# A third split product in two of eight steps, high parts at the ends of cycles, early transforms one product later, two last sends on GpSimd's queue

## The chip, the cores and the metric

One core of one Trainium2 chip runs the whole program. The time is the device time of one execution in microseconds; three executions of the kernel before took 1777.51, 1778.03 and 1778.36 us, so its median is 1778.03 us.

## The reference

```python
X = np.fft.fft(x, axis=1)          # x: (8, 3008, 256) float32
X = np.fft.fft(X, axis=2)
x = X.real.reshape(24064, 256)
h = x @ w_in                       # w_in: (256, 2048)
g = h * np.clip(h + 3.0, 0.0, 6.0) / 6.0
out = g @ w_out                    # w_out: (2048, 256)
```

A two-dimensional Fourier transform over positions and channels is followed, on its real part, by a two-layer network with a hard swish between the layers. All data are float32.

## The kernel before, in words

**The pieces.** The 3008 positions are 47 times 64. `stage1` (L327) transforms over the 47, `stage2` (L563) over the 64, and the transform over the channels is folded into `w_in`. Images go in four pairs, and each pair has 12 chunks of at most 256 columns, so there are 48 chunks. The last chunk of each pair (`ch.last`) has 192 columns in the second layer. A chunk has 8 steps, one for each 256 columns of the hidden layer; `fc` counts them from 0 to 7. Step number s is 8 times the chunk plus `fc`.

**First layer.** From step 22 on, a `Unit` computes 512 columns of the first layer: `passes` (L717) multiplies split parts of the transform (tile KQ) with split parts of the weights (KW) into a bank `u`, first the even half (128 rows, `blk` 0), later the odd half (127 rows, `blk` 1). Between them ScalarE keeps the even sums (`s<-u`, L741) because the odd half goes on adding into the same bank. VectorE then makes the other sign (`v<-s,u`, L751), ScalarE two Relu (`t`, L791), VectorE two gates (`A<-t`, L794).

**Second layer.** It is a Strassen-like scheme: GpSimd combines the four gated blocks of a step (`c`, L809), and `mlp2` (L865) makes seven products i = 0 to 6 into four `acc` banks, 256 columns each. A product in float32 is written in the trace as two matmul records. From chunk 8 on (`CHUNK2`), products 0 and 1 are made of three fp32r matmuls instead: high part, low part and rest of the moving data (tile J, written by `split_gates`, L882 to L893) times high parts of the weights (GH) or their low parts and rests (GK). `THIRD = (4,)` adds product 2 of step 4 of every chunk: `split_third` (L895 to L905) writes tile J3 with two operations on ScalarE (`J<-A` 256 at L900, `high<-J` 256 at L903) and two on VectorE (L904, L905), and the product becomes three fp32r matmuls from J.

**Order.** Nothing is scheduled by a tool; the program is written in cycles by the loop at the end of the kernel. From chunk 8 on one cycle is one step and one unit: odd half of a unit, product 0, product 1, even half of the next unit, any `stage2`, then the other products. Work on the other engines is put between. In a cycle with a `stage1`, its matmuls stand `behind_it` products before the cycle's end: 1 where the step before held a `stage2`, else 2. `third_high()` issues the first operation of a third in the cycle before the step, `third_others()` the other three at the end of that cycle. `split_weights` (L908) makes GK; `keep_high` (L922 to L927) turns the weights GH from float32 to their high parts by two operations on ScalarE through a bank, once per step of chunk 7 that is done, in the middle of a cycle. While one of the two is under way `lent` is set, and `split_gates` then takes bank y0 (shared with `v` and with `split_third`) instead of y1.

**The end.** The last chunk's results go out in `send` (L1026): two tiles of eight DMAs each, alternately issued from SyncE and ScalarE.

**The start.** FI (row indices, a column of signs, and 16-bit tables E) is loaded once, on ScalarE's queue, into a tile that lives through the program.

Of the kernel before, what the change touches and what calls it, by code (L numbers as in the profile page):

```python
# [60 lines left out]
def kernel(  # L61
# [67 lines left out]
    CHUNK2, NFR = 8, 2  # L129
    THIRD = (4,)  # L130
    SPLIT = CHUNK1 * NF - 2
# [5 lines left out]
    F1 = consts.tile([P, 5 * PB], F32, name="F1")  # L137
    FI = consts.tile([P, NIX + 1 + P], F32, name="FI")
    IX = FI[:, 0:NIX].bitcast(I32)
# [4 lines left out]
    G = consts.tile([P, 6 - NFR, NF, P], F32, name="G")  # L144

    def split_products(fc):
        return NFR + (fc in THIRD)

    GH = [consts.tile([P, split_products(fc), P], F32, tag=f"GH{fc}", name="GH") for fc in range(NF)]
    G2 = {fc: consts.tile([P, P], F32, tag=f"G2{fc}", name="G2") for fc in range(NF) if fc not in THIRD}  # L150

    def weight(i, fc):
        if i == NFR and fc in G2:
            return G2[fc][:]
        return GH[fc][:, i] if i <= NFR else G[:, i - NFR - 1, fc]
    half = consts.tile([P, 1], F32, name="half")
# [486 lines left out]
    def split_q(ch, ps):  # L643

        x = ps[:, :, 0:ch.nq]
        high, low, rest = (KQ[:, j, :, ch.n_all % 3, 0:ch.nq] for j in range(3))
        ch.row = qpool.tile([P, TB], F32, tag="row", name="row")
        nc.scalar.mul(high, x, 1.0 - EPS / 2.0)
        nc.scalar.copy(ch.row[P - DH:P, 0:ch.nq], ps[P - DH:P, 1, 0:ch.nq])

        def low_part():
            nc.vector.scalar_tensor_tensor(low, x, 1.0, high.bitcast(F32), op0=AL.mult, op1=AL.subtract)
# [177 lines left out]
    def split_of(ch, fc):  # L830
        return ch.n_all >= CHUNK2

    def order_of(ch, fc):

        if not split_of(ch, fc):
            return [[(i, None)] for i in range(7)]
        high, others = ([(i, j) for i in range(NFR)] for j in (HIGH, OTHERS))
        rest = [[(i, ALL if i < split_products(fc) else None)] for i in range(NFR, 7)]
        if ch.final and fc >= NF - LAST:
            return [high, others] + [rest[i - NFR] for i in (3, 5, 6, 4, 2)]  # L840
        if fc in THIRD:
            rest = rest[1:3] + rest[0:1] + rest[3:]
        order = [high] + rest[:2] + [others] + rest[2:]
        while len(order) > 7:
            order[0:2] = [order[0] + order[1]]
        return order

    def mlp2(ch, fc, lo, hi):
        a = ch.a[fc].rearrange("p m f n -> p (m f) n")[:, :, 0:ch.n]
        c = ch.c[fc]  # L850
        moving = [a[:, 0], a[:, 1], a[:, 3], c[:, 0], c[:, 1], c[:, 2], c[:, 3]]
        order = order_of(ch, fc)
        if fc == NF - 1 and lo == 0:
            ch.e = epool.tile([P, 5, TB], F32, tag="e", bufs=1, name="e")
            if ch.final:
                ch.e2 = epool.tile([P, 2, TB], F32, tag="s", bufs=1, name="e")
        for i, parts in (x for part in order[lo:hi] for x in part):
            if fc == 0 and i % 2 == 0 and parts != OTHERS:
                ch.acc[i // 2] = ps_a.tile([P, 2, TB], F32, tag="acc", name="acc")
            o = ch.acc[i // 2][:, i % 2, 0:ch.n]  # L860
            for j in parts or (None,):
                assert (j is None) != (weight(i, fc).dtype == F32R)
                w = weight(i, fc) if not j else GK[fc][:, j - 1, i]
                x = moving[i] if j is None else J3[:, j, 0:ch.n] if i == NFR else parts_tile(ch, fc)[:, j, i, 0:ch.n]
                nc.tensor.matmul(o, w, x,  # L865
                                 start=(fc == 0 and i % 2 == 0 and j in (None, 0)), stop=(fc == NF - 1),
                                 skip_group_check=True)
# [42 lines left out]
    def split_weights(fc):  # L910

        low, rest = (GK[fc][:, k] for k in range(2))
        ps = bank([P, split_products(fc), P], "high")
        nc.scalar.mul(low, GH[fc][:], HIGH_PART)
        nc.vector.tensor_scalar(ps[:], low.bitcast(F32), 1.0 / EPS, None, op0=AL.mult)
        nc.vector.scalar_tensor_tensor(low, GH[fc][:], (1.0 + EPS) / EPS, ps[:], op0=AL.mult, op1=AL.subtract)
        nc.vector.scalar_tensor_tensor(ps[:], ps[:], -EPS, low.bitcast(F32), op0=AL.mult, op1=AL.add)
        yield
        nc.vector.tensor_scalar(rest, ps[:], 1.0 / (1.0 + EPS), None, op0=AL.mult)

    def keep_high(fc):

        ps = bank([P, split_products(fc), P], "high")
        nc.scalar.copy(ps[:], GH[fc][:])
# [92 lines left out]
    def send(ch, o, m):  # L1017
        if not ch.final:
            for j, (bj, k1) in enumerate(ch.blocks[m]):
                nc.sync.dma_start(out=out_k[ch.pr.p, k1, bj], in_=o[:, j].rearrange("p h e -> p (h e)"))  # L1020
            return
        for j in (slice(0, 4), slice(4, 6)):
            (b0, k1), (b1, _) = ch.blocks[m][j][:2]
            rows = out_k[ch.pr.p, k1, b0::b1 - b0]
            for q in range(P // DH):
                (nc.sync, nc.scalar)[q % 2].dma_start(  # L1026
                    out=rows[:, q].rearrange("b i e -> i b e"),
# [74 lines left out]
    def join(j):  # L1102
# [7 lines left out]

        outs = GH[2 * n + i][:, 0:NFR], G[:, B12 - NFR - 1:B22 - NFR:B22 - B12, 2 * n + i]
        for h, o in enumerate(outs):
# [3 lines left out]
    def mix_w_out(j):  # L1116

        g = {i: G[:, i - NFR - 1, 2 * j:2 * j + 2, :] for i in range(NFR + 1, 7)}
        tt = nc.gpsimd.tensor_tensor
# [4 lines left out]
        for k in range(2):  # L1124
            tt(weight(2, 2 * j + k), g[5][:, k], GH[2 * j + k][:, B21], op=AL.subtract)

# [30 lines left out]


    def load_table():
        nc.sync.dma_start(out=F1[:], in_=c_stage1[:, 8 * PB:13 * PB])  # L1160
# [14 lines left out]
    load_w(0, nc.sync)  # L1175
    nc.scalar.dma_start(out=F[:], in_=c_stage1[:, 0:8 * PB])
    nc.scalar.dma_start(out=FI[:], in_=c_stage1[:, 13 * PB:])
    zero = QN[PB:PX, 2]
# [125 lines left out]
    def beside():  # L1304
# [50 lines left out]
    def open_slots():  # L1355
        nonlocal A, GK
# [3 lines left out]
        GK = [slots.tile([P, 2, split_products(fc), P], F32R, tag=f"GK{fc}", name="GK") for fc in range(NF)]  # L1360

# [4 lines left out]

    epool = jpool = KW = A = GK = J = J3 = None
    steps = [(p, ck, fc) for p in range(NP) for ck in range(NCK) for fc in range(NF)]
# [256 lines left out]
    seed(units[1])  # L1625
    weights_of, rested, kept = list(range(NF)), 0, 0

# [3 lines left out]

    thirds = [s for s in gates_of if steps[s][2] in THIRD]
    third = []

    def third_high():

        if thirds and not third and thirds[0] <= now[0] + 1:
            ch, fc = chunk(thirds.pop(0))
# [50 lines left out]
    while done < len(stream):  # L1689
# [18 lines left out]
        third_high()  # L1708
        if not un:
            third_others()  # L1710

# [56 lines left out]
        flush(high_of)  # L1768
        third_others()
        for gen in parts:  # L1770
            next(gen, None)
# [112 lines left out]
```

## Time and profile before

| what | value |
|---|---|
| median of three executions | 1778.03 us (1777.51 to 1778.36) |
| the profiled execution's own time | 1779.34 us |
| its span, first to last instruction | 1777.5 us |
| granted TensorE clock | 0.999 |
| idle of TensorE ahead of a matmul, named waits, whole program | 2.2, 1.6, 0.9, 0.8, 0.6, 0.5, 0.5, 0.3 us |
| GpSimd's `c` waiting for `acc` products | 330.5 us in 247 waits |

The profiled execution took 1.3 us more than the median, so a sum of pieces of it is a difference to be taken from either. Matmuls are pipelined and their ends are modelled, so the table of busy time says little here: a matmul that starts late because of a wait inside the row is still drawn as busy. What a step costs is read from the starts of equal rows in consecutive cycles.

### The profile page before, as it was taken

The numbers are of one execution on the slowest core, as the hardware profiler recorded it, in microseconds if no ns is written. First come the engines' busy times: TensorE is split into PE (matmuls) and PEld (weight loads), VectorE is DVE, ScalarE is ACT, GpSimd is POOL, SyncE is SP. The second block draws the span as 40 slices with busy tenths as digits, with TensorE's granted clock in tenths as the row PEclk, the third lists the DMA queues.
The fourth block names the chain that finished last, engine by engine and source line by source line (L and its number), as shares of the span: only waits on it lengthen the run. The fifth ranks groups of instructions, "written<-read, shape, count | busy, mean of one in ns | idle before, by whom it ended". The sixth has DMA issues, their size and how long they took to land.

```text
span 1777.5 us, 30218 instructions
## 1 busy us (share of the span) xinstructions
PE 1764.3 (99%) x9632; PEld 1518.3 (85%) x9632; DVE 1494.5 (84%) x2868; ACT 1411.4 (79%) x2573; POOL 1312.7 (74%) x1474
## 2 busy tenths in 40 slices
PE   8999999999999999999999999999999999999998
PEld 6688888888988888888998888888899888888897
DVE  8988676668988888888898888888899888888887
ACT  6556666678888888888888888888888888888885
POOL 5687777776678787886768878887766766776675
PEclk9999999999999999999999999999999999999999
DMA  8433332312113222121112222321111111101101
GB/s 281 121 93 99 103 78 70 85 37 51 37 48 81 71 64 78 47 73 43 30 44 64 70 78 57 86 64 37 48 36 34 37 21 48 41 19 45 21 13 34
DMA packets 160811, 110.39 MB, mean 62 GB/s; under 512 B 122562, under 2 KB 141344, under 8 KB 160652
## 3 DMA queue, kind: packets, MB, share of 16 engines
q1 hardware_dynamic: 151900, 82.22, 18.5%
q0 software_dynamic: 7504, 25.65, 4.7%
q8 instruction: 76, 1.25, 0.3%
q14 instruction: 83, 0.68, 0.1%
q10 hardware_dynamic: 1248, 0.59, 0.1%
HBM read 71.93 MB, written 36.79 MB: 61 GB/s over the span
## 4 chain that ended last, share of the span: by engine, by line
PE 95%; DVE 2%; ACT 2%; issue 0%; DMA 0%; another core or an unknown queue 0%; DVEq 0%; ACTq 0%
PE acc L865 58%; PE u L717 27%; PE ps L563 2%; PE ps L327 2%; PE acc L819 1%; PE v L613 1%; PE u L613 1%; ACT t L791 1%; PE spare L1138 0%; DVE v L751 0%; PE ps L526 0%; PE ps L395 0%; PE awake L1165 0%; DVE J L892 0%; ACT PM L1069 0%
## 5 line engine op out<-in xcount | busy, mean ns | idle before, releaser
L865 PE MATMUL acc<-c,G 128*128 128x256 f32 (+1 forms) x3008 | 766.7, 376 | 0.0
L717 PE MATMUL u<-KQ,KW 128*128 128x512 f32 (+7 forms) x2376 | 743.8, 426 | 1.0 <-ACT s L741 0.6
L809 POOL TENSOR_TENSOR c<-A 128x512 f32<-128x512 f32 (+1 forms) x359 | 453.9, 1264 | 337.3 <-PE acc L865 328.5
L865 PEld LDWEIGHTS acc<-c,G 128*128 128x128 f32 x3008 | 533.1, 189 | 80.3 <-issue 12.8
L717 PEld LDWEIGHTS u<-KQ,KW 128*128 128x128 f32 (+1 forms) x2376 | 426.1, 189 | 67.0 <-ACT s L741 3.0
L791 ACT ACTIVATE t<-u,half 128x512 f32<-128x512 f32 (+1 forms) x384 | 261.9, 682 | 169.9 <-PE u L717 111.7
L791 ACT ACTIVATE t<-v,half 128x512 f32<-128x512 f32 (+1 forms) x384 | 262.3, 683 | 106.1 <-DVE v L751 104.5
L751 DVE SCALAR_TENSOR_TENSOR v<-s,u 128x512 f32<-128x512 f32 (+1 forms) x360 | 247.0, 686 | 117.5 <-ACT t L791 111.6
L809 POOL TENSOR_TENSOR c<-c,A 128x256 f32<-128x256 f32 (+1 forms) x359 | 260.4, 725 | 28.2
L809 POOL TENSOR_TENSOR c<-A,c 128x256 f32<-128x256 f32 (+1 forms) x359 | 260.2, 725 | 28.2
L794 DVE SCALAR_TENSOR_TENSOR A<-t,v 128x512 f32<-128x512 f32 (+3 forms) x481 | 250.2, 541 | 36.7 <-ACT t L791 34.1
L865 PE MATMUL acc<-J,GK 128*128 128x256 f32 (+1 forms) x1340 | 270.7, 322 | 1.4 <-DVE J L905 0.8
L892 DVE SCALAR_TENSOR_TENSOR J<-high,A 128x512 fp32r<-128x512 f32 (+1 forms) x315 | 211.2, 670 | 55.8 <-ACT high L891 45.4
L794 DVE SCALAR_TENSOR_TENSOR A<-t,u 128x512 f32<-128x512 f32 (+3 forms) x481 | 248.4, 537 | 0.0
L732 ACT ACTIVATE u<-QN,WN 128x512 f32<-128x512 f32 (+1 forms) x324 | 224.8, 694 | 0.0
L865 PEld LDWEIGHTS acc<-J,GK 128*128 128x128 f32 x1340 | 204.7, 189 | 17.5 <-DVE J L893 1.6
L893 DVE SCALAR_TENSOR_TENSOR J<-high,A 128x512 fp32r<-128x512 f32 (+1 forms) x315 | 210.5, 668 | 0.0
L886 ACT ACTIVATE J<-A 128x512 fp32r<-128x512 f32 (+1 forms) x315 | 193.4, 614 | 0.0
L891 ACT COPY high<-J 128x512 f32<-128x512 f32 (+1 forms) x315 | 185.2, 588 | 4.9 <-DVE KQ L893 2.4
L741 ACT COPY s<-u 128x512 f32<-128x512 f32 (+2 forms) x315 | 180.3, 572 | 9.5 <-PE u L717 8.3
L865 PE MATMUL acc<-A,G 128*128 128x256 f32 (+1 forms) x630 | 184.6, 375 | 0.0
L865 PEld LDWEIGHTS acc<-J,GH 128*128 128x128 f32 x670 | 125.8, 189 | 24.1
(184 smaller groups left out, 1808.5 us busy)
## 6 DMA issues: line engine op xcount, KB each, us to landing
out_dram<-o SPq DMA_DIRECT2D x744, 32.0 KB
T<-in_c_stage_dram SPq DMA_DIRECT2D x26, 512.0 KB
g<-zd SPq DMA_DIRECT2D x42, 256.0 KB
zd<-z SPq DMA_DIRECT2D x48, 192.0 KB
QN<-qd SPq DMA_DIRECT2D x43, 128.0 KB
xt<-in_x_dram SPq DMA_DIRECT2D x21, 256.0 KB
st<-in_moe_w_out_dram POOLq DMA_DIRECT2D x7, 512.0 KB
xt<-in_x_dram SPq DMA_DIRECT2D x17, 192.0 KB
```

The costliest lines, as they stand in the source:

```text
L717: nc.tensor.matmul(un.wide(un.u[:]) if un.joint else un.u[:, i, 0:un.nq], un.weights(j, blk, i, rows), un.moving(j, blk, rows), start=Fals ...
L732: nc.scalar.activation(un.wide(un.u[:]), un.wide(row), AF.Identity, scale=WN[:, f:f + 1])
L741: copy(un.wide(un.s[:]), un.wide(un.u[:]))
L751: nc.vector.scalar_tensor_tensor(v, s, -2.0, u, op0=AL.mult, op1=AL.add)
L791: nc.scalar.activation(t, h, AF.Relu, bias=half[:], scale=scale)
L794: nc.vector.scalar_tensor_tensor(dst, t, 1.0, h, op0=AL.min, op1=AL.mult)
L809: (eng or nc.gpsimd).tensor_tensor(out, in0, in1, op=AL.add)
L865: nc.tensor.matmul(o, w, x, start=(fc == 0 and i % 2 == 0 and j in (None, 0)), stop=(fc == NF - 1), skip_group_check=True)
L886: nc.scalar.mul(high, a, 1.0 - EPS / 2.0)
L891: nc.scalar.copy(ps, high.bitcast(F32))
L892: nc.vector.scalar_tensor_tensor(low, ps, -1.0, a, op0=AL.mult, op1=AL.add)
L893: nc.vector.scalar_tensor_tensor(rest, ps, 1.0 + EPS, a, op0=AL.mult, op1=AL.subtract)
```

## The change

It has six parts.

1. `THIRD` becomes (3, 5), and the new `third_of` leaves out the last chunks. Product 2 is split in two steps of 36 chunks instead of one step of 40. The order within such a step is as it was for step 4. Weights for it are made by `split_third_weights` into three tiles GK3 of their own, after the eight `split_weights`.
2. `keep_high` is called at the end of a cycle, at most twice, after product 1 of the step concerned has been issued, and uses bank y0; it no longer sets `lent`.
3. `behind_it` is 1 in all steps below 62.
4. The last two of the eight last sends are issued from GpSimd.
5. FI is put in a tile that is freed after step 7, and `load_index` loads its indices and signs again, on SyncE's queue in step 2, into a small tile `signs`.
6. The one-row copy that is spread over the partitions is written straight into QN, and the layout of the weight tiles changes (G2 goes into G, GK is one tile). `third_high()` is also called from `third_others()`, and the early call of `third_others()` in cycles without a unit goes.

```diff
-    THIRD = (4,)
+    THIRD = (3,5)
...
-        ch.row = qpool.tile([P, TB], F32, tag="row", name="row")
+        ch.row = QN[:, ch.n_all % 4]
...
+    def third_of(ch, fc):
+        return split_of(ch, fc) and fc in THIRD and not ch.last
...
-        if fc in THIRD:
-            rest = rest[1:3] + rest[0:1] + rest[3:]
+        rest = [[(i, None)] for i in range(NFR, 7)]
+        if third_of(ch, fc):
+            rest = rest[1:3] + [[(NFR, ALL)]] + rest[3:]
...
+    def split_third_weights(fc):
+        yield from split_parts(weight(NFR, fc), bank([P, P], "high")[:], *(GK3[fc][:, j] for j in range(3)))
...
     def keep_high(fc):
 
-        ps = bank([P, split_products(fc), P], "high")
+        ps = ps_u.tile([P, NFR, P], F32, tag="y0", name="high")
         nc.scalar.copy(ps[:], GH[fc][:])
-        GH[fc] = consts.tile([P, split_products(fc), P], F32R, tag=f"GH{fc}", name="GH")
+        GH[fc] = consts.tile([P, NFR, P], F32R, tag=f"GH{fc}", name="GH")
         nc.scalar.mul(GH[fc][:], ps[:], HIGH_PART)
-        yield
...
-        for j in (slice(0, 4), slice(4, 6)):
+        for i, j in enumerate((slice(0, 4), slice(4, 6))):
...
-                (nc.sync, nc.scalar)[q % 2].dma_start(
+                (nc.sync, nc.scalar, nc.gpsimd)[2 if m == i == 1 and q > 1 else q % 2].dma_start(
...
+    def load_index():
+        nonlocal FI, IX
+        FI, IX = signs, signs[:, 0:NIX].bitcast(I32)
+        nc.sync.dma_start(out=FI[:], in_=c_stage1[:, 13 * PB:13 * PB + NIX + 1])
...
+        put(2, load_index)
...
     def third_others():
+        third_high()
         for gen in third:
             next(gen, None)
...
-        if not un:
-            third_others()
...
-        if kept < NF and not stages and not ends and done >= 7 * ((CHUNK2 - 1) * NF + kept - SPLIT) + 7:
-            splitting, kept = keep_high(kept), kept + 1
-            next(splitting)
-        elif weights_of and not stages and not ends and not closing and rested >= 3:
-            splitting, rested = split_weights(weights_of.pop(0)), 0
+        if weights_of and not stages and not ends and not closing and rested >= 3:
+            (f, fc), rested = weights_of.pop(0), 0
+            splitting = f(fc)
             next(splitting)
...
-        behind_it = 1 if any(s - 1 in middle_fns for s in begun) else 2
+        behind_it = 1 if any(s - 1 in middle_fns or s < CHUNK2 * NF - 2 for s in begun) else 2
...
         third_others()
+        for _ in range(2):
+            if kept < NF and not stages and not ends and done >= 7 * ((CHUNK2 - 1) * NF + kept - SPLIT) + NFR:
+                keep_high(kept)
+                kept += 1
```

What this does to the order of instructions shows in three places.

TensorE, two neighbouring steps of a usual chunk (here chunk 17), from the step's even half of the first layer (the L717 row) on. Before, steps 3 and 4; the products of `c` are those with GpSimd's combinations, J those with split data:

```order
L717 MATMUL u<-KQ,KW 128x512 x3
L865 MATMUL acc<-c,G 128x256
L865 MATMUL acc<-J,GK 128x256 x4
L865 MATMUL acc<-c,G 128x256 x3
L717 MATMUL u<-KQ,KW 128x512 x3
L865 MATMUL acc<-J,GH 128x256 x2
L865 MATMUL acc<-c,G 128x256
L717 MATMUL u<-KQ,KW 128x512 x3
L865 MATMUL acc<-c,G 128x256
L865 MATMUL acc<-J,GK 128x256 x4
L865 MATMUL acc<-J,GH 128x256
L865 MATMUL acc<-J,GK 128x256 x2
```

Now step 3 and the start of step 4:

```order
L709 MATMUL u<-KQ,KW 128x512 x3
L863 MATMUL acc<-c,G 128x256
L863 MATMUL acc<-J,GK 128x256 x4
L863 MATMUL acc<-J,GK_1680 128x256 x3
L863 MATMUL acc<-c,G 128x256 x2
L709 MATMUL u<-KQ,KW 128x512 x3
L863 MATMUL acc<-J,GH 128x256 x2
L863 MATMUL acc<-A,G 128x256
```

The three extra fp32r matmuls now follow the four of products 0 and 1 in step 3 (and again in step 5), and step 4 has its product 2 in float32 once more (the row `A,G`).

ScalarE, from the end of chunk 8's step 2 to the end of its step 3. `high<-GH` and `GH<-high` are `keep_high`, `J<-A` 256 and `high<-J` 256 the third. Before:

```order
L924 COPY high<-GH 128x256
L926 ACTIVATE GH<-high 128x256
L891 COPY high<-J 128x512
L732 ACTIVATE u<-QN,WN 128x512
L791 ACTIVATE t<-u,half 128x512
L886 ACTIVATE J<-A 128x512
L900 ACTIVATE J<-A 128x256
L791 ACTIVATE t<-v,half 128x512
L741 COPY s<-u 128x512
L924 COPY high<-GH 128x256
L926 ACTIVATE GH<-high 128x256
L891 COPY high<-J 128x512
```

Now, from the last two `keep_high`, at the end of step 0 of that chunk, to the end of step 1:

```order
L724 ACTIVATE u<-QN,WN 128x512
L927 COPY high<-GH 128x256
L929 ACTIVATE GH<-high 128x256
L927 COPY high<-GH 128x256
L929 ACTIVATE GH<-high 128x256
L783 ACTIVATE t<-u,half 128x512
L884 ACTIVATE J<-A 128x512
L783 ACTIVATE t<-v,half 128x512
L733 COPY s<-u 128x512
L889 COPY high<-J 128x512
```

The high parts of all eight steps are now made by the end of step 0 of chunk 8; steps 1 to 3 hold none, where before steps 0 to 3 held one each, ahead of the step's own copy `high<-J`.

TensorE, a cycle with a `stage1` in chunk 3 (`ps<-y`), before:

```order
L865 MATMUL acc<-A,G_112 128x256
L327 MATMUL ps_1871<-y,F_97 64x512
L327 MATMUL ps_1872<-y,F_97 64x512
L327 MATMUL ps_1871<-y,F_97 64x512
L327 MATMUL ps_1872<-y,F_97 64x512
L865 MATMUL acc<-c,G 128x256 x2
```

and now:

```order
L863 MATMUL acc<-A,G 128x256
L863 MATMUL acc<-c,G 128x256
L319 MATMUL ps_1860<-y,F_97 64x512
L319 MATMUL ps_1861<-y,F_97 64x512
L319 MATMUL ps_1860<-y,F_97 64x512
L319 MATMUL ps_1861<-y,F_97 64x512
L863 MATMUL acc<-c,G 128x256
```

One product has moved ahead of the transform. This happens in four cycles with a `stage1` (two in chunk 3, one each in chunks 5 and 6); the others below step 62 had `behind_it` 1 already.

More of the change, by code (lines that the diff above doesn't have):

```diff
@@ L143 @@
     WN = consts.tile([P, NFC], F32, name="WN")
[L144 to L150, printed above, removed]
+    G = consts.tile([P, 7 - NFR, NF, P], F32, name="G")
+    GH = [consts.tile([P, NFR, P], F32, tag=f"GH{fc}", name="GH") for fc in range(NF)]
     def weight(i, fc):
-        if i == NFR and fc in G2:
-            return G2[fc][:]
-        return GH[fc][:, i] if i <= NFR else G[:, i - NFR - 1, fc]
+        return GH[fc][:, i] if i < NFR else G[:, i - NFR, fc]
     half = consts.tile([P, 1], F32, name="half")
@@ L837, in order_of @@
         high, others = ([(i, j) for i in range(NFR)] for j in (HIGH, OTHERS))
-        rest = [[(i, ALL if i < split_products(fc) else None)] for i in range(NFR, 7)]
         if ch.final and fc >= NF - LAST:
-            return [high, others] + [rest[i - NFR] for i in (3, 5, 6, 4, 2)]
-        if fc in THIRD:
-            rest = rest[1:3] + rest[0:1] + rest[3:]
+            return [high, others] + [[(i, None)] for i in (3, 5, 6, 4, 2)]
+        rest = [[(i, None)] for i in range(NFR, 7)]
+        if third_of(ch, fc):
+            rest = rest[1:3] + [[(NFR, ALL)]] + rest[3:]
         order = [high] + rest[:2] + [others] + rest[2:]
@@ L861, in mlp2 @@
             for j in parts or (None,):
-                assert (j is None) != (weight(i, fc).dtype == F32R)
-                w = weight(i, fc) if not j else GK[fc][:, j - 1, i]
-                x = moving[i] if j is None else J3[:, j, 0:ch.n] if i == NFR else parts_tile(ch, fc)[:, j, i, 0:ch.n]
+                w, x = weight(i, fc), moving[i]
+                if parts and i == NFR:
+                    w, x = GK3[fc][:, j], J3[:, j, 0:ch.n]
+                elif parts:
+                    w, x = GK[:, j - 1, fc, i] if j else w, parts_tile(ch, fc)[:, j, i, 0:ch.n]
+                assert (j is None) != (w.dtype == F32R)
                 nc.tensor.matmul(o, w, x,
@@ L1116, in mix_w_out @@
     def mix_w_out(j):
-        g = {i: G[:, i - NFR - 1, 2 * j:2 * j + 2, :] for i in range(NFR + 1, 7)}
+        g = {i: G[:, i - NFR, 2 * j:2 * j + 2, :] for i in range(NFR, 7)}
         tt = nc.gpsimd.tensor_tensor
@@ L1355, in open_slots @@
     def open_slots():
-        nonlocal A, GK
+        nonlocal A, GK, GK3
         ectx.__exit__(None, None, None)
@@ L1359, in open_slots @@
         A = slots.tile([P, NSLOT, 2, 2, TB], F32, name="A")
-        GK = [slots.tile([P, 2, split_products(fc), P], F32R, tag=f"GK{fc}", name="GK") for fc in range(NF)]
+        GK = slots.tile([P, 2, NF, NFR, P], F32R, name="GK")
+        GK3 = {fc: slots.tile([P, 3, P], F32R, tag=f"GK{fc}", name="GK3") for fc in THIRD}
     def open_parts():
@@ L1625 @@
     seed(units[1])
-    weights_of, rested, kept = list(range(NF)), 0, 0
+    weights_of = [(split_weights, fc) for fc in range(NF)] + [(split_third_weights, fc) for fc in THIRD]
+    rested, kept = 0, 0
     def turn_before(s):
         return s - (3 if chunk(s)[0].final and steps[s][2] else 1)
-    thirds = [s for s in gates_of if steps[s][2] in THIRD]
+    thirds = [s for s in gates_of if third_of(*chunk(s))]
     third = []
@@ L1637, in third_high @@
         if thirds and not third and thirds[0] <= now[0] + 1:
+            assert thirds[0] > now[0]
             ch, fc = chunk(thirds.pop(0))
```

26 lines of the change are left out of this document (14 added, 12 removed).

## The prediction

> **What bounds the kernel now.** I read the page's busy shares first, then TensorE's timeline step by step, and last the timelines of VectorE and ScalarE at the places that the change touches.
>
> ```profile
> PE 1764.3 (99%) x9632; PEld 1518.3 (85%) x9632; DVE 1494.5 (84%) x2868; ACT 1411.4 (79%) x2573; POOL 1312.7 (74%) x1474
> PE 95%; DVE 2%; ACT 2%; issue 0%; DMA 0%; another core or an unknown queue 0%; DVEq 0%; ACTq 0%
> ```
>
> TensorE is busy throughout and the chain that ended last is 95% TensorE. So a saving counts only if it takes matmuls or waits off TensorE, and work on the others is free until TensorE waits for it. Busy time can't show such waits, since a row is drawn as busy over a short one. Equal rows in consecutive cycles can: each cycle begins with the odd half, `127x512 f32 x3`. TensorE in chunk 17:
>
> ```profile
> 712.31 1.03 PE L717 MATMUL u<-KQ,KW 127*128 127x512 f32 x3
> ...
> 716.57 1.05 PE L717 MATMUL u<-KQ,KW 127*128 127x512 f32 x3
> ...
> 719.72 0.28 PE L865 MATMUL acc<-J,GH 128*128 128x256 f32 x1
> 719.84 0.40 PE L865 MATMUL acc<-J,GK 128*128 128x256 f32 x2
> ...
> 720.75 0.59 PE L717 MATMUL u<-KQ,KW 127*128 127x512 f32 x1
> ```
>
> The step without a third takes 716.57 - 712.31 = 4.26 us, the one with it (rows 719.72 and 719.84) 720.75 - 716.57 = 4.18 us. One third of 256 columns is thus worth 0.08 us, all waits included.
>
> **1. The second third.** Before, 36 full chunks had one; now they have two, in steps 3 and 5: 36 more at 0.08 us are **2.9 us**. This holds if the splitting behind it stays hidden, so the cover has to be looked at. VectorE, then ScalarE, around the third of before:
>
> ```profile
> 714.11 0.70 DVE L751 SCALAR_TENSOR_TENSOR v<-s,u 128x512 f32<-128x512 f32 x1 [0.37 <-ACT t L791]
> ...
> 717.73 0.41 DVE L904 SCALAR_TENSOR_TENSOR J<-high,A 128x256 fp32r<-128x256 f32 x1
> 718.06 0.41 DVE L905 SCALAR_TENSOR_TENSOR J<-high,A 128x256 fp32r<-128x256 f32 x1
> 718.58 0.70 DVE L751 SCALAR_TENSOR_TENSOR v<-s,u 128x512 f32<-128x512 f32 x1
> ```
>
> ```profile
> 715.42 0.58 ACT L741 COPY s<-u 128x512 f32<-128x512 f32 x1
> ...
> 717.04 0.37 ACT L903 COPY high<-J 128x256 f32<-128x256 f32 x1
> ...
> 719.90 0.58 ACT L741 COPY s<-u 128x512 f32<-128x512 f32 x1
> ```
>
> The copy `s<-u` must end before TensorE's next odd half. In the step without a third it ends at 716.00, 0.57 us ahead of the 716.57 row; in the step with one at 720.48, 0.27 us ahead of 720.75. The two operations on VectorE take 0.74 us (717.73 to 718.47), but `v` starts only 0.21 us later in its step (2.01 instead of 1.80 us after the odd half), because VectorE had 0.37 us of idle time before `v` and takes the rest out of `v`'s own slack. The copy on ScalarE (717.04) has no wait ahead of it. Behind the delayed `v` stand the gates, behind them the next copies and the seed of the next bank; 0.27 us is what is left. Step 2's end now gets what step 3's end had, with the same transpose of finished results in front; step 4's end has no such transpose. I take the cover as whole; what it costs if it is gone is a rival below.
>
> One place differs. In the next-to-last chunk of three pairs a second-stage transform stands in step 4, so its split (L652) meets the new third at that step's end. VectorE, ScalarE and TensorE in chunk 10:
>
> ```profile
> 474.92 0.68 DVE L652 SCALAR_TENSOR_TENSOR KQ<-ps,KQ 128x512 fp32r<-128x512 f32 x1
> 475.51 0.56 DVE L751 SCALAR_TENSOR_TENSOR v<-s,u 128x388 f32<-128x388 f32 x1
> ```
>
> ```profile
> 476.59 0.58 ACT L741 COPY s<-u 128x512 f32<-128x512 f32 x1
> ```
>
> ```profile
> 477.83 1.03 PE L717 MATMUL u<-KQ,KW 127*128 127x512 f32 x3
> ```
>
> There is no idle time ahead of `v` here, so 0.74 us move it fully. The copy ends at 477.17, 0.66 us early; the delay and the 0.08 us by which the step gets shorter leave -0.16 us, and the following step starts late too. Bounds: 0 and twice the delay, 1.5 us, for each. I take 0.3, near the computed end: **-0.9 us** for the three.
>
> The weights for it are ten operations on 128 columns in chunks 6 and 7. If nothing hid the eight on VectorE, each at most the 0.41 us of a 256-column row, it would be 3.3 us; they lie in cycles without any J work, so I cost them at nothing.
>
> **2. No third in last chunks.** Chunk 11, of 192 columns, steps 3 and 4 on TensorE; and the last chunk of all:
>
> ```profile
> 497.55 0.96 PE L717 MATMUL u<-KQ,KW 127*128 127x512 f32 x3
> ...
> 501.26 0.96 PE L717 MATMUL u<-KQ,KW 127*128 127x512 f32 x3
> ...
> 505.36 0.97 PE L717 MATMUL u<-KQ,KW 127*128 127x512 f32 x3
> ```
>
> ```profile
> 1764.28 0.47 PE L865 MATMUL acc<-J,GK 128*128 128x192 f32 x2 [0.84 <-DVE J L905]
> ```
>
> With the third the step takes 4.10 us, without it 3.71: it costs 0.39 us there, three times, 1.17 us. In the last chunk TensorE waits 0.84 us for L905 alone; other waits stand close behind, so I count 0.7. Together **1.9 us**.
>
> **3. High parts at cycles' ends.** Chunk 8, steps 2, 3 and 4, on TensorE, and ScalarE there:
>
> ```profile
> 387.61 1.05 PE L717 MATMUL u<-KQ,KW 127*128 127x512 f32 x3
> ...
> 392.10 1.05 PE L717 MATMUL u<-KQ,KW 127*128 127x512 f32 x3
> ...
> 396.60 1.03 PE L717 MATMUL u<-KQ,KW 127*128 127x512 f32 x3
> ...
> 402.19 0.96 PE L717 MATMUL u<-KQ,KW 127*128 127x512 f32 x3 [0.63 <-ACT s L741]
> ```
>
> ```profile
> 396.33 0.39 ACT L924 COPY high<-GH 128x256 f32<-128x256 f32 x1
> ...
> 398.98 0.38 ACT L903 COPY high<-J 128x256 f32<-128x256 f32 x1 [0.74 <-DVE J L893]
> ```
>
> The three steps take 4.49, 4.50 and 5.59 us where 4.26, 4.26 and 4.18 are usual: 0.23 + 0.24 + 1.41 = 1.88 us too long. The cause is in the second fence: each step held a `keep_high` (two operations of 0.39 us), and because `lent` was set, the split's bank was y0, for which the third's copy waited 0.74 us with `t<-u` behind it. Now steps 1 to 3 hold none and `lent` is not set. What is late next is the four operations at the end of step 0: 4 x 0.39 = 1.56 us ahead of `t<-u`. But `v` needs the seed and `s`, not `t<-u`, and late by ScalarE's idle time less, so I keep 0.1 us of stall: **1.8 us**. Bounds: 0 (it all comes back at step 1) and 1.9.
>
> **4. Early transforms one product later.** TensorE in two of the four cycles concerned, and one that already has the new order:
>
> ```profile
> 183.58 0.59 PE L865 MATMUL acc<-A,GH 128*128 128x256 f32 x2
> 184.01 0.59 PE L865 MATMUL acc<-A,G 128*128 128x256 f32 x2
> 184.54 2.10 PE L327 MATMUL ps<-y,F 47*64 47x512 f32 x8
> ```
>
> ```profile
> 307.02 1.69 PE L327 MATMUL ps<-y,F 47*64 47x512 f32 x8
> ```
>
> ```profile
> 373.30 1.09 PE L327 MATMUL ps<-y,F 47*64 47x512 f32 x8
> ```
>
> The eight records last 1.09 us where they run freely and 1.69 to 2.10 in the cycles concerned: they wait inside for a bank that VectorE's second gate frees. That moment does not depend on their place, so a product of 0.43 us (183.58 to 184.01) put ahead of them fits into the wait, which is at least 0.60 us: 4 x 0.43 = **1.7 us**. Bounds 0 and 1.7.
>
> **5. Two last sends on GpSimd.**
>
> ```profile
> 1773.35 1.82 ACTq L1026 DMA_DIRECT2D out_dram<-o  x4
> ```
>
> ```profile
> L422 POOL DMA_DIRECT2D g<-z x8 | 4.4, 558 | 5.7 <-ACT z L403 3.3 <-issue 1.4 <-ACT z L405 0.9
> ```
>
> ```profile
> g<-z POOLq DMA_DIRECT2D x8, 32.1 KB, 3.4
> ```
>
> Four issues take 1.82 us, 0.46 each, and the span ends 2.3 us behind the last one. With three the hardware queues end 0.46 us earlier: that is the gain if GpSimd's two land in time. A GpSimd issue takes 0.56 us and landed 3.4 us after it began, in the crowded first 25 us. The second would begin at about 1773.9 and land at 1777.3; its worst end is that plus the 2.3, 1779.6, 2.1 us later. From +0.5 to -2.1 I take **-0.3 us**, nearer the quiet end.
>
> The Trainium skill, "DMA: Bandwidth & Descriptors", section "Anatomy of one DMA — SWDGE (gpsimd) path", puts a DMA from GpSimd at about 2.0 us plus its bytes at 436 GB/s. For 16 KB this is an estimate of 2.04 us, so the second send would land near 1775.9 and the term would be +0.46 us instead of -0.3. The 3.4 us row is longer, but no row has such a send on quiet queues.
>
> **6. The rest.** `load_index` is one more issue (0.46 us) on SyncE's queue, ahead of the loads of WN.
>
> ```profile
> SPq L1128 <- ACT W L1146: 8.2, 4, 4.8
> ```
>
> The queue waits up to 4.8 us there for ScalarE, so it is hidden; uncovered it would delay the WN column by 0.46 us. The row copy into QN and the weight layouts change no count of instructions, and the dropped early `third_others()` only served the last chunk, which has no third now.
>
> **The sum.** 2.9 - 0.9 + 1.9 + 1.8 + 1.7 - 0.3 = 7.1 us. Against the profiled execution's 1779.34 us that is 1772.2; it ran 1.3 us over the median of 1778.03, so the median becomes **1770.9 us**, 0.40% faster.
>
> **The rivals.**
>
> *The stalls only move.* The high parts' 1.56 us come back at step 1 of chunk 8, and the early transforms' cycles wait for a later link. Terms 3 and 4 vanish: 7.1 - 3.5 = 3.6 us, 1774.4 us. For it: VectorE and ScalarE are at 84% and 79%. Against it: the 1.09 row, and the named `s` wait tied to `lent`.
>
> *The cover of the thirds is gone.* If `v` were moved by the full 0.74 us at step 2's end, the 0.57 us of step 3 would become 0.57 - 0.74 - 0.08 = -0.25 us in 36 chunks, 9.0 us lost: 1770.9 + 9.0 = 1779.9, no change that can be told. Against it stands the present third, which moves `v` by 0.21 us.
>
> *Bank y0 in every chunk (slower).* If the split's bank at the ends of steps 2 and 4 were y0 as at 398.98, the third's copy would wait 0.74 us with `t<-u` behind it, against 0.27 us of slack: 0.47 us in 36 chunks, 16.9 us, giving 1787.8. It decides from 0.20 us a chunk, where the 7.1 are eaten. Against it: the copy at 717.04 waits for nothing, and y0 is taken only where a second-stage split is unfinished.
>
> *The thirds bring nothing but cost nothing*, because the step is bound elsewhere: 7.1 - 2.9 = 4.2, 1773.8.
>
> **How the numbers follow.** The forecast (1768.5 to 1772.8 by the bounds of its terms) has 0.66; stalls moving 0.15; thirds without gain 0.07; cover gone 0.06; bank y0 0.06. The range for 8 in 10 takes in the first two and reaches from **1768.3 to 1774.5**. A measurement of this kernel can tell about 0.2%, 3.6 us, from no change: faster means under 1774.5. That has the forecast, the thirds without gain and most of the moved stalls: 0.87; the same 0.07; slower 0.06.
>
> **What would show each step.** Steps 3 and 5 of a usual chunk about 4.18 us after their odd half and step 4 back at 4.26 (term 1); idle ahead of TensorE's odd halves named `s` would refute it. Step 4 of chunk 11 at about 3.7 us and no 0.84 us wait near the end (2). Steps 2 to 4 of chunk 8 near 4.2 us, without the wait at 402.19 (3). Early transforms' rows of about 0.43 us less (4). The end of the span less than 2.3 us behind the last hardware issue, or later by GpSimd (5). The prediction is wrong if a wait that no row of before shows repeats in every chunk: 0.1 us in each of 36 is half the gain.

## The result and the profile after

The changed kernel took 1773.09 us (median of nine executions, 1772.07 to 1774.26), the kernel before 1778.10 in the same session (nine, 1777.03 to 1778.65). The ratio is 0.9972, 95% interval 0.9962 to 0.9983: 5.0 us or 0.28% faster. The forecast was 7.1 us, or 1770.9; 1773.09 lies in its range for 8 in 10. The profiled execution took 1773.9 us with a span of 1772.1, 5.4 us less than before. All line numbers below are those of the changed kernel, where helpers have moved: `passes` is L709, `mlp2` L863, `s<-u` L733, the split of the second stage L644, `keep_high` L927 and L929, `send` L1028.

Engines and chain on the page of after:

```profile
PE 1760.0 (99%) x9664; PEld 1518.6 (86%) x9664; DVE 1514.1 (85%) x2940; ACT 1430.2 (81%) x2639; POOL 1314.2 (74%) x1476
PE 97%; DVE 1%; DMA 1%; ACT 1%; issue 0%; POOL 0%; POOLq 0%; DVEq 0%; ACTq 0%
```

VectorE has 19.6 us more work than before and TensorE's chain share has risen from 95 to 97%, so the added work did not become the limit. POOL and POOLq are in the chain now; they stand at its very end.

TensorE in chunk 17, rows of step 3 (with a third) and step 4 (without):

```profile
707.33 1.03 PE L709 MATMUL u<-KQ,KW 127*128 127x512 f32 x3
...
709.80 1.19 PE L863 MATMUL acc<-J,GK 128*128 128x256 f32 x7
...
711.51 1.05 PE L709 MATMUL u<-KQ,KW 127*128 127x512 f32 x3
...
713.99 0.82 PE L863 MATMUL acc<-J,GK 128*128 128x256 f32 x4
...
715.75 1.03 PE L709 MATMUL u<-KQ,KW 127*128 127x512 f32 x3
```

Seven instead of four fp32r records mark the third. Its step takes 711.51 - 707.33 = 4.18 us, the other 4.24. The rival of bank y0 in every chunk is gone too: of the 72 copies `high<-J` of a third, 69 wait for nothing. The other three are those in the meetings with L644, and wait 0.73 us each (chunk 10's row):

```profile
470.65 0.38 ACT L901 COPY high<-J 128x256 f32<-128x256 f32 x1 [0.73 <-DVE J L891]
```

The step that holds this wait lasts no longer than usual, as is worked out further down.

TensorE in chunk 8, odd halves of steps 1 to 5:

```profile
381.15 1.05 PE L709 MATMUL u<-KQ,KW 127*128 127x512 f32 x3
...
385.71 0.97 PE L709 MATMUL u<-KQ,KW 127*128 127x512 f32 x3
...
389.88 1.03 PE L709 MATMUL u<-KQ,KW 127*128 127x512 f32 x3
...
394.06 1.05 PE L709 MATMUL u<-KQ,KW 127*128 127x512 f32 x3
...
398.31 1.03 PE L709 MATMUL u<-KQ,KW 127*128 127x512 f32 x3
```

Steps 2 to 4 take 4.17, 4.18 and 4.25 us in place of 4.49, 4.50 and 5.59. Step 1 takes 4.56 instead of 4.25 us: a part of the stall came back there.

TensorE in chunk 11, steps 3 and 4, now without a third, and its last named wait in the last chunk:

```profile
493.52 0.95 PE L709 MATMUL u<-KQ,KW 127*128 127x512 f32 x3
...
497.23 0.96 PE L709 MATMUL u<-KQ,KW 127*128 127x512 f32 x3
```

```profile
1758.78 0.70 PE L863 MATMUL acc<-KQ,GK 128*128 128x192 f32 x4 [0.26 <-DVE KQ L891]
```

Step 3 takes 497.23 - 493.52 = 3.71 us; step 4, up to the next odd half at 500.94, takes as long, in place of 4.10. In the last chunk the 0.84 us wait is gone, and one of 0.26 us stands behind it.

The early transform of chunk 3, whose row lasted 2.10 us before, lasts 0.44 less:

```profile
184.67 1.66 PE L319 MATMUL ps<-y,F 47*64 47x512 f32 x8
```

The end, all engines' timeline of after (SPq and ACTq are DMA issues of the hardware queues; the POOL row is its two sends):

```profile
1762.60 3.30 SPq L1028 DMA_DIRECT2D out_dram<-o  x7
1762.61 3.38 ACTq L1028 DMA_DIRECT2D out_dram<-o  x7
...
1764.22 0.38 DVE L1017 STREAM_TRANSPOSE o<-e 128x192 f32<-128x192 f32 x1
1764.90 1.19 POOL L1028 DMA_DIRECT2D out_dram<-o  x2 [5.92 <-DVE o L1017]
```

The last transpose ends at 1764.60. Before, it ended at 1773.32 and the span 4.22 us behind it; now the span ends 7.50 us behind it. So the change had won 8.72 us when the results were ready, and lost 3.28 on the way out. The last hardware issue ended 0.46 us earlier relative to the transpose, as forecast, so the loss is not on those queues. What stands there is found by asking for the closing line of the program (L1879 before, L1893 after) on GpSimd. "POOLq DRAIN" is an instruction of its sequencer, drawn from before the end of the engine's last work until some time behind it; the three figures are its duration in ns, then its start. Before:

```profile
L1879 POOLq DRAIN  x1: 5712/5712/5712, 1766.5 to 1766.5; - x1
```

and after:

```profile
L1893 POOLq DRAIN  x1: 5960/5960/5960, 1765.4 to 1765.4; - x1
L1893 POOLq EVENT_SEMAPHORE  x1: 17/17/17, 1771.4 to 1771.4; - x1
```

The drain was in the kernel before too. It ended at 1772.24 us there, 4.5 us ahead of SyncE's (1776.77), so it did not set the end. After, it ends at 1771.31, 3.0 us behind SyncE's (1768.33), and the last semaphores follow it. Yet the sends themselves had landed 3.7 us before, by 1767.63. The row of the DMA view gives KB each and the median time from issue to landing:

```profile
out_dram<-o POOLq DMA_DIRECT2D x2, 16.0 KB, 2.0
```

The landing is not quite free either. SyncE's closing waits:

```profile
L1893 SPq EVENT_SEMAPHORE  x12: 17/28/28, 1767.7 to 1772.0; - x12
```

They begin at 1767.65, 0.02 us behind that landing, and ten of them, 0.06 us apart, lead to SyncE's drain, which ends 3.73 us behind the last transpose. Before, it was 3.45. So SyncE's end did not gain the 0.46 us of the earlier issue but lost 0.28, hidden behind GpSimd's drain.

### The profile page after: what moved, and what is told of

Read it like the earlier page. It is cut to its first block, busy times and chain, and to the rows that moved or that the text cites. A ratio compares the mean times of both kernels' runs of the same rounds, so it can differ in the third digit from the quotient of the medians.

```text
span 1772.1 us, 30458 instructions
## 1 busy us (share of the span) xinstructions
PE 1760.0 (99%) x9664; PEld 1518.6 (86%) x9664; DVE 1514.1 (85%) x2940; ACT 1430.2 (81%) x2639; POOL 1314.2 (74%) x1476
## 3 DMA queue, kind: packets, MB, share of 16 engines
q8 instruction: 76, 1.25, 0.3%
## 4 chain that ended last, share of the span: by engine, by line
PE 97%; DVE 1%; DMA 1%; ACT 1%; issue 0%; POOL 0%; POOLq 0%; DVEq 0%; ACTq 0%
PE acc L863 60%; PE u L709 28%; PE ps L555 2%; PE ps L319 2%; PE acc L811 1%; PE v L605 1%; PE u L605 1%; DMA xt<-in_x_dram,IT 1%; PE spare L1140 0%; PE ps L518 0%; PE wps L1140 0%; ACT PM L1071 0%; PE ex L1085 0%; PE ps L425 0%; POOL xt L208 0%
## 5 line engine op out<-in xcount | busy, mean ns | idle before, releaser
L863 PE MATMUL acc<-c,G 128*128 128x256 f32 (+1 forms) x3008 | 772.6, 376 | 0.0
L709 PE MATMUL u<-KQ,KW 128*128 128x512 f32 (+7 forms) x2376 | 743.0, 426 | 0.0
L863 PEld LDWEIGHTS acc<-c,G 128*128 128x128 f32 x3008 | 531.5, 189 | 77.8 <-issue 13.7
L709 PEld LDWEIGHTS u<-KQ,KW 128*128 128x128 f32 (+1 forms) x2376 | 426.1, 189 | 64.1 <-ACT s L733 1.0
L863 PE MATMUL acc<-J,GK 128*128 128x256 f32 (+1 forms) x1476 | 282.4, 319 | 0.5 <-DVE J L891 0.5
L863 PEld LDWEIGHTS acc<-J,GK 128*128 128x128 f32 x1476 | 217.9, 189 | 16.4 <-DVE J L891 1.1
L733 ACT COPY s<-u 128x512 f32<-128x512 f32 (+2 forms) x315 | 180.3, 572 | 9.1 <-PE u L709 7.9
L863 PE MATMUL acc<-A,G 128*128 128x256 f32 (+1 forms) x576 | 168.2, 374 | 0.0
L863 PEld LDWEIGHTS acc<-J,GH 128*128 128x128 f32 x630 | 118.3, 189 | 23.7
```

The source lines that it names most:

```text
L709: nc.tensor.matmul(un.wide(un.u[:]) if un.joint else un.u[:, i, 0:un.nq], un.weights(j, blk, i, rows), un.moving(j, blk, rows), start=Fals ...
L733: copy(un.wide(un.s[:]), un.wide(un.u[:]))
L863: nc.tensor.matmul(o, w, x, start=(fc == 0 and i % 2 == 0 and j in (None, 0)), stop=(fc == NF - 1), skip_group_check=True)
```

## The experiments

The ratios below are each to the kernel before in the same session; 0.001 is 1.8 us.

**Where the 3.3 us at the end come from.** Theory D: GpSimd's closing drain takes about 5 us behind GpSimd's last work, whatever that is.

*All sends on the hardware queues.*

```diff
-                (nc.sync, nc.scalar, nc.gpsimd)[2 if m == i == 1 and q > 1 else q % 2].dma_start(
+                (nc.sync, nc.scalar)[q % 2].dma_start(
```

> The changed kernel with all eight last sends on the two hardware queues, as before (part 4 of the change undone). In the changed kernel the last transpose of VectorE ends at 1764.60 us of a span of 1772.1, in the kernel before at 1773.32 of 1777.5: 8.7 us ahead there, 5.4 at the end. Theory D (GpSimd's closing drain): it ends 5.2 us behind GpSimd's second send and alone sets the end, so without the two sends the span ends 4.2 us behind the last transpose, as before: 3.3 us less than the changed kernel, about 1769.8 us, 0.9953 of the kernel before. Rival L (the two sends land late): the packets end at 1766.9, before SyncE's own end, so this would give at most 0.5 us, about 1772.6. Rival E (the tail is late for another reason, such as the end's semaphores): no change, 1773.1.

Measured: 1769.67 us (1769.43 to 1770.59), ratio 0.9954 (0.9940 to 0.9968). That is theory D's number; rival E falls, and rival L explains no more than the 0.38 us by which SyncE's drain is now nearer to the last transpose (3.35 us instead of 3.73). The drain on GpSimd:

```profile
L1893 POOLq DRAIN  x1: 5698/5698/5698, 1758.1 to 1758.1; - x1
```

It ends at 1763.83, hidden again. The span, 1768.5 us, ends 4.13 us behind the last transpose. All its runs lie below all of either kernel's (after's were taken in another session), and it is the base of the later runs.

*The two sends alone, on the kernel before.* The edit is the reverse of the one above.

> The kernel before with only the two last sends moved to GpSimd's queue. Theory D: the drain, which ends at 1772.24 us in the kernel before and is hidden there, moves behind the second send and ends the span: 3.3 us later, about 1781.4 us, 1.0018 of the kernel before. Rival L: within 0.5 us of it. By the forecast's own term (0.3 us) it would be 1778.4.

Measured: 1781.40 us (1780.42 to 1783.56), ratio 1.0022 (1.0013 to 1.0031). The part alone makes the kernel slower. In its trace the drain ends at 1778.46 and the span at 1779.25, 7.50 us behind the last transpose.

```profile
L1879 POOLq DRAIN  x1: 5960/5960/5960, 1772.5 to 1772.5; - x1
```

*One send instead of two* (`q > 2` in place of `q > 1`).

> The changed kernel with one send instead of two on GpSimd's queue. Theory D (the drain ends about 5.2 us behind GpSimd's last instruction, whatever its kind and number): the only send ends 0.6 us earlier, so the span is 0.6 us shorter than the changed kernel's, 1772.5 us. Rival S (each send costs its own share of the drain, 2.6 us each behind the landing): 2.6 us shorter, about 1770.5.

Measured: 1772.85 us (1771.94 to 1774.86), ratio 0.9974 (0.9963 to 0.9984). The span ends 6.83 us behind the last transpose, 0.67 less than with two sends and 2.70 more than with none: the first send carries most of the price, as theory D has it; rival S had put it at half.

```profile
L1893 POOLq DRAIN  x1: 5768/5768/5768, 1763.9 to 1763.9; - x1
```

*No send, but a last small copy on GpSimd.*

```diff
-                (nc.sync, nc.scalar, nc.gpsimd)[2 if m == i == 1 and q > 1 else q % 2].dma_start(
+                (nc.sync, nc.scalar)[q % 2].dma_start(
...
+        if m == 1:
+            nc.gpsimd.tensor_copy(half[:], o[:, 5, 1, 0:1])
```

> All eight last sends on the hardware queues, and one added copy of 128x1 on GpSimd that reads the last transposed tile (it writes a constant that nothing reads any more). Theory D: the drain belongs to any last instruction of GpSimd, not to a send; the copy ends near 1764.8 us, the drain near 1769.9, the span near 1770.7: 1.8 us more than the version without the copy and 1.4 less than the changed kernel, about 1771.7 us. Rival S (the drain is the price of a DMA from GpSimd): the same as the version without the copy, about 1769.8.

Measured: 1772.11 us (1770.93 to 1772.31), ratio 0.9966 (0.9952 to 0.9980). GpSimd's row and its drain:

```profile
1764.20 0.19 POOL L1032 COPY half<-o 128x1 f32<-128x1 f32 x1 [5.12 <-DVE o L1017]
```

```profile
L1895 POOLq DRAIN  x1: 5273/5273/5273, 1764.2 to 1764.2; - x1
```

The drain ends at 1769.46, and the span 5.53 us behind the last transpose instead of 4.13, by a copy of 0.19 us that nobody reads. It waited for an earlier transpose than the last, and ends 0.33 us ahead of the last one's end (1764.39 to 1764.72), where the second send ends 1.49 us behind it: hence it costs less than two sends, and less than the 1.8 us expected. The drain belongs to the engine, not to the DMA; rival S falls.

*The two sends 2 us earlier*, from the first of the two last tiles (`2 if i > m and q > 1`).

> The changed kernel with GpSimd taking two sends of the first last group (ready 2.0 us earlier) in place of two of the second. Theory D: the drain ends 5.2 us behind the second of them, so the two cost as much less as they are issued earlier: 3.3 - 2.0 = 1.3 us more than with all sends on the hardware queues (1769.67 us, 0.9954 of the kernel before), 1771.0 us. Rival S (the price of a send lies behind its landing at the very end): nothing is left, 1769.7. Rival (fixed price wherever a send from GpSimd stands near the end): 1773.1.

Measured: 1771.65 us (1770.98 to 1772.06), ratio 0.9957 (0.9943 to 0.9971). The ratio alone doesn't separate it from the version without sends. Its trace does:

```profile
1762.71 1.19 POOL L1028 DMA_DIRECT2D out_dram<-o  x2 [3.91 <-DVE o L1017]
```

```profile
L1893 POOLq DRAIN  x1: 5960/5960/5960, 1763.2 to 1763.2; - x1
```

The span ends 5.48 us behind the last transpose, between 4.13 and 7.50: the cost is a matter of when GpSimd ends, as theory D has it.

From the event times of the traces, in us (GpSimd's last work is its last combination, copy or send):

| kernel | last work ends | drain ends | between | SyncE's drain ends | span |
|---|---|---|---|---|---|
| before | 1767.17 | 1772.24 | 5.08 | 1776.77 | 1777.54 |
| all hardware | 1758.76 | 1763.83 | 5.08 | 1767.73 | 1768.51 |
| small copy | 1764.39 | 1769.46 | 5.08 | 1768.08 | 1770.25 |
| one send | 1764.49 | 1769.63 | 5.14 | 1766.92 | 1770.42 |
| two sends, earlier | 1763.91 | 1769.13 | 5.22 | 1767.93 | 1769.92 |
| after | 1766.09 | 1771.31 | 5.22 | 1768.33 | 1772.10 |
| two sends on before | 1773.23 | 1778.46 | 5.22 | 1775.46 | 1779.25 |

In every row the span ends 0.8 us behind the later of the two drains.

**What the other parts are worth.** Each is undone on the version with all sends on the hardware queues, where the tail is as before. The sizes are read from the starts of TensorE's rows, since the medians are uncertain by 1 to 2 us; each is then from one trace of each kernel.

*One third, in step 4* (`THIRD = (4,)`, last chunks still without).

> The version with all eight last sends on the hardware queues (1769.67 us, 0.9954 of the kernel before), but with one third, in step 4, as before. Theory: a second third is worth 0.08 us in each of 36 full chunks and costs nothing where a split of the second stage meets it, so 36 x 0.08 = 2.9 us are lost: 1772.6 us, 0.9970 of the kernel before; steps 3 and 5 again last 4.26 us, step 4 4.18. Rival (the forecast's -0.9 us for the three meetings with L652 is there): only 2.0 us are lost, 1771.7. Rival (a third without gain): 1769.7.

Measured: 1773.69 us (1773.30 to 1779.54), ratio 0.9976 (0.9966 to 0.9986). The ratio alone holds both sizes. In the traces steps 3, 4 and 5 differ by +2.56, -2.41 and +2.82 us over all chunks, 2.97 together; the meetings with L644 cost nothing.

*High parts in the middle of the steps, as before:*

```diff
-        ps = ps_u.tile([P, NFR, P], F32, tag="y0", name="high")
+        ps = bank([P, NFR, P], "high")
...
+        yield
...
-        for _ in range(2):
-            if kept < NF and not stages and not ends and done >= 7 * ((CHUNK2 - 1) * NF + kept - SPLIT) + NFR:
-                keep_high(kept)
-                kept += 1
...
+        if kept < NF and not stages and not ends and done >= 7 * ((CHUNK2 - 1) * NF + kept - SPLIT) + 7:
+            splitting, kept = keep_high(kept), kept + 1
+            next(splitting)
```

> The version with all eight last sends on the hardware queues, but the high parts of the weights are kept where the kernel before kept them (in the middle of the steps of chunk 8, with the split's bank lent). Theory: the stalls of chunk 8 come back, 1.7 us: 1771.4 us, 0.9963 of the kernel before, with steps 2 to 4 of chunk 8 together about 1.9 us over their usual time and step 1 without the 0.3 us that it lost. Rival (the stalls only moved): 1769.7.

Measured: 1772.18 us (1771.77 to 1773.12), ratio 0.9966 (0.9952 to 0.9979). TensorE in chunk 8, odd halves of steps 2 to 5, then ScalarE's copy in step 3:

```profile
384.81 1.05 PE L709 MATMUL u<-KQ,KW 127*128 127x512 f32 x3
...
389.28 1.05 PE L709 MATMUL u<-KQ,KW 127*128 127x512 f32 x3
...
394.87 0.97 PE L709 MATMUL u<-KQ,KW 127*128 127x512 f32 x3 [0.63 <-ACT s L733]
...
399.48 1.03 PE L709 MATMUL u<-KQ,KW 127*128 127x512 f32 x3
```

```profile
391.65 0.38 ACT L901 COPY high<-J 128x256 f32<-128x256 f32 x1 [0.74 <-DVE J L891]
```

The long step, 394.87 - 389.28 = 5.59 us, and its 0.74 us wait are back, now in step 3, where the third is. Steps 2 and 4, which hold a high part and no third, take 4.47 and 4.61 us. A wait of the third's copy is not enough by itself: in the meetings with L644 it waits 0.73 us and the step stays at 4.17. So the long stall needs the third and the high part with its lent bank in one step; which of the high part's two effects, its operations or the bank, weighs more there is not shown. Against the base, steps 1 to 4 together lose 1.71 us, and 0.28 more comes in step 6, where the `stage1` row lasts 1.53 us instead of 1.25.

*The last two high parts spread over two steps* (at most one per step once chunk 8 has begun).

> All eight last sends on the hardware queues, and the last two high parts kept at the ends of two steps (steps 0 and 1 of chunk 8) in place of one. Theory: two operations of 0.39 us ahead of a gate fit into what ScalarE has free, four did not, so step 1 of chunk 8 loses its 0.3 us and nothing comes back at step 2: 0.3 us less, 1769.4 us. Rival: step 2 takes 0.1 to 0.3 us longer and nothing is gained, 1769.7.

Measured: 1769.89 us (1769.54 to 1770.39), ratio 0.9948 (0.9934 to 0.9961), not to be told from 0.9954. TensorE in chunk 8, odd halves of steps 1 to 3:

```profile
380.94 1.05 PE L709 MATMUL u<-KQ,KW 127*128 127x512 f32 x3
...
385.19 1.03 PE L709 MATMUL u<-KQ,KW 127*128 127x512 f32 x3
...
389.45 1.05 PE L709 MATMUL u<-KQ,KW 127*128 127x512 f32 x3
```

Step 1 takes 4.25 us instead of 4.56, step 2 4.26 instead of 4.20 in the base. So four operations of 0.39 us did not fit and two do: 0.25 us net, seen in one trace only.

*Early transforms one product earlier, as before* (`behind_it` without its second condition).

> The version with all eight last sends on the hardware queues, but with the early first-stage transforms one product earlier, as before. Theory: the four cycles of the early transforms get 0.43 us longer each, and one more 0.18: 1.9 us, 1771.6 us, 0.9964 of the kernel before. Rival (the wait only moved to a later link): 1769.7.

Measured: 1772.03 us (1771.73 to 1772.43), ratio 0.9963 (0.9950 to 0.9977). The four cycles are longer by 0.43, 0.44, 0.43 and 0.43 us, 1.73 together; the expected 0.18 in one more cycle did not come. The row of chunk 3 is back at its length:

```profile
184.29 2.09 PE L319 MATMUL ps<-y,F 47*64 47x512 f32 x8
```

*Thirds in last chunks too* (`not ch.final` in place of `not ch.last`).

> The version with all eight last sends on the hardware queues, but with thirds in steps 3 and 5 of the three pairs' last chunks too (192 columns; not in the very last chunk). Theory: a third of 192 columns costs what step 4 of chunk 11 showed, 4.10 - 3.71 = 0.39 us, so six cost 2.3 us: 1772.0 us, 0.9966 of the kernel before. Rival (the 0.39 us belonged to step 4's own neighbours and not to the size): about 0, 1769.7 us.

Measured: 1772.14 us (1772.07 to 1773.87), ratio 0.9967 (0.9955 to 0.9979). The six cost 0.34 to 0.39 us each, 2.18 together. TensorE in chunk 11, odd halves around step 3:

```profile
492.84 0.95 PE L709 MATMUL u<-KQ,KW 127*128 127x512 f32 x3
...
495.06 1.06 PE L863 MATMUL acc<-J,GK 128*128 128x192 f32 x7
...
496.93 0.97 PE L709 MATMUL u<-KQ,KW 127*128 127x512 f32 x3
```

The matmuls cost the same either way at 192 columns: by the starts of consecutive records, 2 x 0.163 us in float32 against 3 x 0.113 in fp32r. The 0.38 us are a gap of 0.47 instead of 0.09 us ahead of the next odd half. ScalarE's `s<-u` there ends 0.05 us before that row, 496.88 to 496.93:

```profile
496.30 0.58 ACT L733 COPY s<-u 128x512 f32<-128x512 f32 x1
```

That is the forecast's rival of the lost cover, in the steps that would take 3.71 us; at 4.18 us it does not appear.

## Why the prediction was right, and where it was not

The total came out in the range partly by luck: misses of opposite sign left 1.7 us between them in the profiled executions (5.4 of 7.1) and 2.1 in the medians. Up to the last transpose the terms summed to 7.4 us and the traces show 8.72; the end was put at -0.3 and was -3.28. The 1768.5 to 1772.8 that the forecast gives as the bounds of its terms do not follow from them (the best ends together give about 8.9 us, 1769.1), and 1773.09 lies just outside. The median alone would also fit the rivals at 1773.8 and 1774.4; only the starts of the rows, stage by stage, rule them out.

| term | forecast, us | before and after | undone alone |
|---|---|---|---|
| 1, second third | 2.9 | 2.8 | 2.97 |
| 1, meetings with L652 (now L644) | -0.9 | 0 | 0 |
| 2, chunk 11 three times, last chunk | 1.17 + 0.7 | 1.14 + 0.52 | 2.18 for six |
| 3, high parts | 1.8 | 1.67 | 1.99 with step 6 |
| 4, early transforms | 1.7 | 1.74 | 1.73 |
| 5, sends on GpSimd | -0.3 | -3.28 | -3.37 |

What is left up to the transpose, 0.85 us, has no part of the change to its name: 0.31 lies ahead of the first regular cycle, whose start says nothing, since it lay between 165.75 and 167.07 us in the runs with the changed head and at 165.75 and 167.32 in the two with the old one. 0.18 lies in one early cycle, which did not come back when term 4 was undone, and the rest is spread over steps that nothing was meant to change.

**Term 5** failed in this step: "its worst end is that plus the 2.3". It took the end of the span to hang on landings only. The sends landed in 2.0 us, faster than the 3.4 us of the row used, and the end that hangs on landings, SyncE's drain, moved by -0.28 us: near the -0.3, though not by its working. That was not the last end. The end also waits for each engine's drain, and GpSimd's takes 5.1 to 5.2 us behind its last work. The row for it was in the trace of before (5712 ns), with 4.5 us to spare; the sends moved its end from 1.1 us ahead of the last transpose to 6.7 us behind it. The term was worked out from issue times and landing times, and the question what else closes the program was not asked. The measured loss lies outside the bounds given (+0.46 to -2.1). The hardware queues did issue 0.46 us earlier, but SyncE then waited for GpSimd's landings, so none of it reached the end.

On the 2.0 us: the Trainium skill, "DMA: Bandwidth & Descriptors", section "Anatomy of one DMA — SWDGE (gpsimd) path", puts such a DMA at about 2.0 us plus its bytes at 436 GB/s, an estimate of 2.04 us for 16 KB. This trace agrees with it: 1.92 and 2.13 us. The sum made by it, +0.46 us, was further off than the one made by the row, since even that landing was later than the last one of the hardware queues (1767.63 against 1767.43), and GpSimd's drain later still.

**The meetings with L652** failed in taking start times out of before. VectorE, ScalarE and TensorE of after, in chunk 10, step 4's end:

```profile
469.33 0.69 DVE L890 SCALAR_TENSOR_TENSOR J<-high,A 128x512 fp32r<-128x512 f32 x1 [0.98 <-ACT high L889]
...
470.54 0.68 DVE L644 SCALAR_TENSOR_TENSOR KQ<-ps,KQ 128x512 fp32r<-128x512 f32 x1
471.13 0.41 DVE L902 SCALAR_TENSOR_TENSOR J<-high,A 128x256 fp32r<-128x256 f32 x1
471.46 0.41 DVE L903 SCALAR_TENSOR_TENSOR J<-high,A 128x256 fp32r<-128x256 f32 x1
471.98 0.57 DVE L743 SCALAR_TENSOR_TENSOR v<-s,u 128x388 f32<-128x388 f32 x1
```

```profile
473.07 0.58 ACT L733 COPY s<-u 128x512 f32<-128x512 f32 x1
```

```profile
469.62 1.00 PE L709 MATMUL u<-KQ,KW 127*128 127x194 f32 x6
...
473.79 1.05 PE L709 MATMUL u<-KQ,KW 127*128 127x512 f32 x3
```

The step runs from 469.62 to 473.79, 4.17 us. Before, L652 began 1.32 us behind the odd half that opened the step; now it begins 0.92 behind. The step ahead, which had held the old third, holds none now, and VectorE comes to this one 0.40 us earlier. So `v` was moved by 0.45 us, not by 0.74, and the copy `s<-u` still ends at 473.65, 0.14 us ahead of TensorE's row. The same change that put a third here took one away in front of it, and the sum counted only the first. This is read from start times; no run puts a third here and leaves the one in front. The sum also had the third's copy without a wait here, where it waits 0.73 us for its bank; the step had room for that too.

**Term 1** stood as worked out, with a thinner cover than forecast: ScalarE's `s<-u` in chunk 17's step 3 ends 0.09 us ahead of the 711.51 row, where 0.27 was the estimate.

```profile
710.84 0.58 ACT L733 COPY s<-u 128x512 f32<-128x512 f32 x1
```

**Term 3**: the mechanism was right, with 0.31 us coming back at step 1 where 0.1 was allowed; spread over two steps it is gone. **Term 2**: the last chunk gave 0.52 of the 0.7 us, with the 0.26 us wait behind the old one. The ten operations for the new weights, costed at nothing, cost nothing that shows. **Term 4** was exact: the transforms' waiting hides the product put ahead of them. That what they wait for is VectorE's second gate was argued, not tested.

## What to carry to other kernels

Ask of every instruction near a program's end what else ends behind it, on its engine as well as in its queue: an engine that had finished early may close the program once it is given a last, small task. When a step is moved, take start times in the neighbouring steps from the new order, since what leaves one step gives time to the next. A sum that comes out right can hold two wrong terms; only the starts of equal rows, stage by stage, and the parts undone one at a time show it.

## What the runs showed of the hardware

All of this is from this one program. GpSimd's closing drain lasted until 5.07 to 5.08 us behind its last computing instruction in the eight kernels without a late send (the shortest of these instructions, a copy of 0.19 us), 5.14 behind one send and 5.22 behind two. TensorE's ended 0.05 us behind its last row in the kernel before (1772.44 to 1772.48, a modelled end), VectorE's 0.05 (1773.32 to 1773.37). A 128x1 copy on GpSimd near the end therefore made the span end 1.4 us later behind the last transpose (5.53 instead of 4.13). From start to start, a matmul record of fp32r took 0.113 us at 192 columns and 0.119 at 256, one of float32 0.163 and 0.216: at 192 columns three of the one cost what two of the other do, at 256 they save 0.08 us.
